# GateLoop and SwiGLU on one core: decays of the first chunks through selection tiles, two units' gates in turns, one weights piece behind the second rows

## The chip, the cores and the metric

One core of a Trainium2 chip runs the whole program. The metric is the device time in microseconds of one execution, as the median of three runs. TensorE is PE in the profile, VectorE DVE, ScalarE ACT, GpSimd POOL, and SyncE (which only issues transfers here) SP.

## What is computed

A gated linear recurrence (GateLoop) is followed by a feed-forward layer with a SwiGLU. Four sequences, eight heads, 768 steps, 48 features per head; then 3072 tokens of width 384, with 1536 hidden features.

```
mag = sqrt(a_re**2 + a_im**2)
a = (a_re + i*a_im) * min(mag, 0.999) / (mag + 1e-6)
for t in range(S):
    state = a[t] * state + outer(k[t], v[t])        # per head, complex
    y[t] = q[t] @ real(state)
x = y, heads side by side: (B*S, 384)
xn = x / sqrt(mean(x*x) + 1e-6) * rms_g
out = (silu(xn @ w_gate) * (xn @ w_val)) @ w_out
```

## The kernel before

The 3072 steps are 24 chunks of 128 steps, six to a sequence. Chunks are worked on in units: chunk 0 is unit 0, chunk 1 is unit 1, and from chunk 2 on two chunks make a unit (`UNITS`, L688). Two chunks also make a feed-forward group, of 256 tokens.

`gates(u)` (from L1011) turns the decays of a unit into rotated and scaled q and k. In stages it squares the real and imaginary parts, takes the reciprocal root, multiplies magnitudes up along the chunk by scans (`t4`), takes their reciprocal root (`root`), takes the half angle by Arctan (stage "turn"), sums angles by scans, takes sine and cosine (`turns`), and multiplies k and q by them into `rot`. Six transfers on SP's queue then spread each chunk's `rot` (features of all heads mixed on 128 partitions) to `kq` (96 partitions for a head's real and imaginary part): the chunk's "rows", noted in `moved`. The decay over a whole chunk, one number per feature and head, is `ends`; six more small transfers on SP spread it to `decay`.

ScalarE evaluates by function tables; a change of table is an ACT_TABLE_LOAD in the profile. The functions of the root, the Arctan, and the Sin are in different tables.

`attend(n)` (L1101) is a chunk's attention: scores of `kq` in blocks into two banks of PSUM, masked into `am` by VectorE's COPY_PREDICATED; transposes of k into `kt`; the products of `am` with `ve` (v with padding) and of q with `state`; the new state from `vn` and `kt`, times `decay`. Then the norm: ScalarE squares the output (`sq`), TensorE sums it, VectorE makes `ssv`, GpSimd takes the power (`rs`), TensorE spreads it over the partitions, VectorE multiplies into `xT`. With both chunks' `xT` a group's feed-forward `feed(g, xT)` (L1222) can start: per block, lists of six products with `wg` and with `wv`, Silu into `sg`, a product into `hT`, and last the products with `wo`.

The weights come as 64-bit floats in twelve pieces, through POOL's queue: 0 and 1 are the first of wg and wv, 2 and 3 the second, 4 and 5 the third, 6 to 11 are wo. `fetch` (L905) issues piece i once piece i-2 has landed; a one-element copy into `junk` on POOL marks the landing. `narrow` (L926) makes 32-bit floats of it: one conversion on ScalarE (128 x 1536) and three steps on VectorE, a shift, a masking step, and an addition (the custom operation on 128 x 3072 words). Three places hold raw pieces in turn, so piece 3 takes the place of piece 0, piece 4 that of 1, piece 5 that of 2. `CLEAR = {3: 0}` (L903) also holds piece 3 until the rows of chunk 0 have landed (`cleared`, a small POOL copy into `seen`).

The order of all instructions comes from a planner (`Flow`, `schedule` at L555): each operation has a planned duration, dependencies taken from the memory that it touches, and a due time worked out backwards; on each engine the planner takes the ready operation that is due first. All instructions are emitted at one line (L667), so groups in the profile are told apart by tile names. Where TensorE would be idle in the first 62 us by plan, the planner puts filler products of `rot` into bank 3 (`flow.warm`, L1338).

At the top level (L1298) `gates(0)` and `gates(1)` are recorded one after the other, then the narrowing of all pieces, then the chunks in turn. The functions follow.

Of the kernel before, what the change touches and what calls it, by code (L numbers as in the profile page):

```python
# [18 lines left out]
P = 128  # L19
# [442 lines left out]
class Flow:  # L462
# [9 lines left out]
    turn = 0.0  # L472
    BEGIN = {"SP": 0.8, "ACT": 0.8, "POOL": 0.8}
# [30 lines left out]
    def note(self, op, ap, write):  # L504
        b = self.box(ap)
        if b is None:
            return
        name, p0, p1, lo, hi = b
        if name.startswith("bank"):
            p0, p1, lo, hi = 0, P, 0, 2048  # L510
        kept = []
        for x in self.seen.get(name, ()):
            o, w, q0, q1, l, h = x
            over = q0 < p1 and p0 < q1 and l < hi and lo < h
            if over and (write or w) and o != op["i"]:
                op["deps"].add(o)
            if not (write and p0 <= q0 and q1 <= p1 and lo <= l and h <= hi):
                kept.append(x)
        kept.append((op["i"], write, p0, p1, lo, hi))
        self.seen[name] = kept  # L520

    def add(self, eng, calls, dur, reads=(), writes=(), table=None, land=None, due=None, after=(), behind=(), late=None, mode=None):
        op = dict(i=len(self.ops), eng=eng, calls=calls, dur=dur, deps=set(), table=table, land=land,
                  base=due, late=late, mode=mode, stage=self.stage, behind={o["i"] for o in behind})
# [30 lines left out]
    def schedule(self):  # L555
# [33 lines left out]
        while True:  # L589
# [36 lines left out]
            o = pick[1]  # L626
            waiting[eng].remove(o)
# [8 lines left out]
            if eng == "PE" and self.warm and t < self.warm["until"]:  # L636
# [33 lines left out]
def fast(tc, ctx, qT, kT, v, a_re, a_im, w_gate, w_val, w_out, rms_g, out, H, bad):  # L670
# [209 lines left out]
    for t in banks[4:6]:  # L880
        fill(t, 0.0, eng="DVE")
    dma(gcol, rms_g.rearrange("(c p) -> p c", p=P))
# [20 lines left out]
    CLEAR = {3: 0}  # L903
# [63 lines left out]
    begun = []  # L967
    started = []
# [5 lines left out]
    def way_of(u):  # L974
        return u if u < 2 else 2 + u % 2
# [26 lines left out]
    def load_kq(u, t):  # L1002
        flow.stage = "kq", u
        for name, ap in (("q", qT), ("k", kT)):
            for i, n in enumerate(UNITS[u]):
                dma(t[name][:, :, i * C:(i + 1) * C],
                    ap[n].rearrange("d (h t) -> (d h) t", t=C).rearrange("(j p) t -> p j t", p=P),
                    behind=moved[HOLD] if u > 1 else rows_)
        return t

    def gates(u):  # L1011
# [46 lines left out]

        flow.stage = "turn", u
        act(im, im, AF.Arctan, after=[root])  # L1060
# [28 lines left out]
        for r in range(2 * ND):  # L1089
            dma(decays[way_of(u)][r:D2:2 * ND], ends[:, r % ND, ns[0]:ns[0] + nt], behind=moved[ns[0]])  # L1090
# [10 lines left out]
    def attend(n):  # L1101
# [4 lines left out]
        later = dict(behind=moved[min(n - 1, HOLD)] if n else ())  # L1106
# [191 lines left out]
    gates(0)  # L1298
    gates(1)
# [3 lines left out]
    for n in range(N):  # L1303
        while gated < NU and UNITS[gated][0] <= n:
            gates(gated)
            gated += 1
# [14 lines left out]
    o = 0  # L1321
# [71 lines left out]
```

## Time and profile before

| | |
|---|---|
| runs | 728.84, 729.06, 732.99 us; median 729.06 |
| the profiled execution's own time | 729.62 us |
| its span, first to last instruction | 727.9 us |
| mean granted TensorE clock | 0.99 |
| busy in the span | PE 685.7 us, DVE 471.6, ACT 334.1, POOL 42.0 |

The profile is of one execution. Its page has the busy time of each engine, the span in 40 slices of 18.2 us (a digit is a tenth of the slice), the transfers, and the chain of work that ended last. A timeline line gives start and length in us, engine, operation, the tile written and those read, and in brackets how long the engine stood idle before it and what ended that. "x6" is six instructions run together in a line. A line of a stretch gives its bounds, length, TensorE's busy time, the clock granted to TensorE as a share of full speed, and the transfers' load.

### The profile page before, as it was taken

To read this page: it belongs to the slowest core of one execution; us is meant where nothing else is said; L and a number is where in the kernel's file an instruction comes from. 1 tells how busy PE (TensorE), PEld (TensorE's weight loads), DVE (VectorE), ACT (ScalarE), POOL (GpSimd) and SP (SyncE) were. 2 spreads that over 40 slices of the span, in tenths; PEclk is the share of its full clock that TensorE was granted. 3 is DMA by queue.
4 is the path that set the end of the run, shared out by engine and by line. 5 is a ranking of instruction groups with operands and counts; after the bars stand their busy time and mean duration, and the time that the engine had idled before them with its cause. 6 is when DMAs were issued, how large, how long until landed. Compare 5 with 4: busy or idle time off the path is not lost.

```text
span 727.9 us, 16198 instructions
## 1 busy us (share of the span) xinstructions
PE 685.7 (94%) x6906; PEld 603.7 (83%) x6906; DVE 471.6 (65%) x740; ACT 334.1 (46%) x452; POOL 42.0 (6%) x80
## 2 busy tenths in 40 slices
PE   0579999999999999999999999999999999999996
PEld 0558867877899889889899889889889889889885
DVE  6979988789897887787847737756745234134121
ACT  7649756755656765732923823822821110110010
POOL 6123100001000000000000000000000000000000
PEclk9979999999999999999999999999999999999999
DMA  8797655634545435543722303314303102200000
GB/s 285 226 304 208 193 168 170 184 106 130 170 127 147 153 93 131 171 153 99 189 82 62 97 20 91 97 34 106 81 17 73 55 12 68 65 13 2 23 1 26
DMA packets 104575, 80.64 MB, mean 111 GB/s; under 512 B 42800, under 2 KB 95280, under 8 KB 104496
## 3 DMA queue, kind: packets, MB, share of 16 engines
q1 hardware_dynamic: 100432, 64.99, 32.8%
q0 software_dynamic: 3264, 14.16, 5.5%
q8 instruction: 56, 0.92, 0.5%
q10 hardware_dynamic: 800, 0.39, 0.2%
q14 instruction: 23, 0.19, 0.1%
HBM read 55.84 MB, written 4.72 MB: 83 GB/s over the span
## 4 chain that ended last, share of the span: by engine, by line
PE 87%; DVE 5%; DMA 3%; ACT 2%; SPq 1%; issue 1%; POOL 0%; DVEq 0%; ACTq 0%
PE bank L667 87%; DMA kq<-rot 2%; SPq L667 1%; DVE turns L667 1%; DVE rot L667 1%; DVE wg L667 1%; ACT t L667 1%; DMA in<-in_a_re_dram 1%; ACT turns L667 0%; DVE t L667 0%; DVE wo L667 0%; DVE wv L667 0%; ACT L667 0%; DVE ot L667 0%; DVE in L667 0%
## 5 line engine op out<-in xcount | busy, mean ns | idle before, releaser
L667 PE MATMUL bank<-xT,wg 128*128 128x256 f32 x864 | 199.8, 381 | 1.6 <-DVE xT L667 1.5
L667 PE MATMUL bank<-xT,wv 128*128 128x256 f32 x864 | 199.1, 380 | 0.0
L667 PEld LDWEIGHTS bank<-xT,wg 128*128 128x128 f32 x864 | 163.7, 191 | 24.5 <-DVE xT L667 2.2
L667 PEld LDWEIGHTS bank<-xT,wv 128*128 128x128 f32 x864 | 163.5, 190 | 22.5
L667 PE MATMUL bank<-wo,hT 128*128 128x192 f32 (+1 forms) x576 | 125.8, 362 | 0.4 <-DVE hT L667 0.4
L667 DVE TENSOR_TENSOR hT<-bank,sg 128x512 f32<-128x512 f32 x72 | 49.6, 689 | 114.4 <-PE bank L667 102.0
L667 PEld LDWEIGHTS bank<-wo,hT 128*128 128x128 f32 x576 | 95.6, 191 | 13.7 <-issue 2.5
L667 ACT ACTIVATE sg<-bank 128x512 f32<-128x512 f32 x72 | 42.9, 596 | 132.0 <-PE bank L667 131.4
L667 ACT ACT_TABLE_LOAD x69 | 88.5, 1283 | 11.5 <-DVE rot L667 7.9
L667 ACT ACTIVATE sq<-bank 128x384 f32<-128x384 f32 x24 | 11.8, 490 | 101.2 <-PE bank L667 101.2
L667 DVE TENSOR_TENSOR rot<-kin,turns 128x768 f32<-128x768 f32 x48 | 44.8, 953 | 14.9 <-DMA kq<-rot 14.5
L667 POOL TENSOR_TENSOR rs<-ssv,mhalf 128x1 f32<-128x1 f32 x24 | 17.2, 717 | 575.4 <-DVE ssv L667 575.4
L667 ACT ACTIVATE kt<-bank 128x384 f32<-128x384 f32 x40 | 18.4, 488 | 60.0 <-PE bank L667 59.8
L667 PE MATMUL bank<-sums,hT 128*128 128x192 f32 x240 | 45.0, 329 | 0.0
L667 ACT ACTIVATE turns<-in 128x768 f32<-128x768 f32 (+1 forms) x39 | 29.9, 789 | 21.0 <-DVE rot L667 12.5
L667 PEld LDWEIGHTS bank<-sums,hT 128*128 128x128 f32 x240 | 39.5, 190 | 0.0
L667 PEld LDWEIGHTS bank<-kq 96*32 96x32 f32 x1536 | 30.3, 111 | 10.4 <-issue 7.7
L667 DVE COPY_PREDICATED am<-causal,bank 128x512 f32<-128x512 int32 x48 | 33.3, 722 | 8.4 <-PE bank L667 8.4
L667 DVE TENSOR_TENSOR hT<-hT 128x768 f32<-128x768 f32 x40 | 38.2, 954 | 0.9
L667 PE MATMUL bank<-am,ve 128*32 128x128 f32 x768 | 38.1, 281 | 0.0
L667 PE MATMUL bank<-kq 96*32 96x96 f32 (+3 forms) x1536 | 34.7, 238 | 3.6 <-DMA kq<-rot 3.6
L667 PE MATMUL bank<-rot 128*128 128x128 f32 x64 | 11.7, 342 | 24.8 <-DVE rot L667 24.8
(112 smaller groups left out, 750.5 us busy)
## 6 DMA issues: line engine op xcount, KB each, us to landing
kq<-rot SPq DMA_DIRECT2D x144, 128.0 KB, 2.4
kin<-in_q_dram SPq DMA_DIRECT2D x24, 192.0 KB, 2.8
kin<-in_k_dram SPq DMA_DIRECT2D x24, 192.0 KB, 3.6
wo<-in_w_gate_dram SPq DMA_DIRECT2D x6, 768.0 KB, 4.6
out_dram<-ot SPq DMA_DIRECT2D x24, 192.0 KB, 2.3
wo<-in_w_val_dram SPq DMA_DIRECT2D x6, 768.0 KB, 5.7
wo<-in_w_out_dram SPq DMA_DIRECT2D x6, 768.0 KB, 5.4
in<-in_a_re_dram SPq DMA_DIRECT2D x11, 384.0 KB, 4.6
```

The costliest lines, as they stand in the source:

```text
L667: fn(*args, **kw)
```

## The change

- The decays of chunks 0 and 1 no longer go by transfers. `ends` of the chunk is multiplied by a small 0/1 tile (`head`) into `own`, three products with the selection tile `pick` spread it to 96 partitions in bank 0 or 1, and VectorE copies it to `decay`. The tiles lie in `ot0` and `ot1`, which are written first by the feed-forward; they are made at the start, by a fill and three copies on POOL and two reductions on VectorE. Other units keep the six transfers.
- `gates` becomes a generator that stops once, ahead of the Arctan; for units 0 and 1 both first parts are recorded, then both second parts, and the Arctan waits for both roots (`roots[-2:]`).
- `CLEAR` is `{3: 1}`: piece 3 waits for the rows of chunk 1.
- The planner: loads of q and k of a unit, and of v of a chunk, form groups whose members don't depend on each other; ScalarE and VectorE may wait a little for an operation that is due over 50 us earlier (`patient`); fillers are planned only once the operations that they wait for are placed.

```diff
+    patient = ("ACT", "DVE")
...
-            if over and (write or w) and o != op["i"]:
+            if over and (write or w) and o != op["i"] and (not op["group"] or self.ops[o]["group"] != op["group"]):
                 op["deps"].add(o)
...
+            if eng in self.patient:
+                for x in waiting[eng]:
+                    if t < ready[x["i"]] < t + o["dur"] - 0.2 and x["due"] < o["due"] - 50.0 and ready[x["i"]] < t + 1.5:
+                        pick = None
+                        free[eng] = max(free[eng], min(ready[y["i"]] for y in waiting[eng] if t < ready[y["i"]]))
+                        break
+                if pick is None:
+                    continue
...
-            if eng == "PE" and self.warm and t < self.warm["until"]:
+            if eng == "PE" and self.warm and t < self.warm["until"] and all("end" in x for x in self.warm["after"]):
...
+    pick = ots[0][:, 0:ND * D2].rearrange("p (r x) -> p r x", r=ND)
+    band, head = (ots[1][:, o:o + n] for o, n in ((0, P // H), (16, H)))
+    own = [ots[1][:, o:o + ND * H].rearrange("p (r h) -> p r h", r=ND) for o in (32, 64)]
+    fill(pick, 0.0, late=LATE)
+    for o, order in ((band, "p (x h) -> p x h"), (head, "p (x h) -> p h x")):
+        add("DVE", [(nc.vector.tensor_reduce, (), dict(out=o, in_=ident.rearrange(order, h=H), axis=mybir.AxisListType.X,
+                                                       op=ALU.add))], 0.3, [ident], [o], late=LATE)
+    for r in range(ND):
+        o = pick[:, r].rearrange("p (x j) -> p x j", j=2 * ND)[:, :, r::ND]
+        copy(o, band.unsqueeze(2).to_broadcast([P, P // H, 2]), eng="POOL", late=LATE)
...
-    CLEAR = {3: 0}
+    CLEAR = {3: 1}
...
+    def send_decays(u):
+        ns = UNITS[u]
+        if u < 2:
+            tt(own[u], ends[:, :, u:u + 1].to_broadcast([P, ND, H]), head.unsqueeze(1).to_broadcast([P, ND, H]))
+            ps = banks[u][0:D2, 0:H]
+            mms([(ps, pick[:, r], own[u][:, r], r == 0, r == ND - 1) for r in range(ND)], 0.5)
+            copy(decays[u][:, :, 0], ps)
+            return
+        for r in range(2 * ND):
+            dma(decays[way_of(u)][r:D2:2 * ND], ends[:, r % ND, ns[0]:ns[0] + len(ns)], behind=moved[max(ns[0], 1)])
...
+        roots.append(root)
+        yield
         flow.stage = "turn", u
-        act(im, im, AF.Arctan, after=[root])
+        act(im, im, AF.Arctan, after=roots[-2:])
...
-        for r in range(2 * ND):
-            dma(decays[way_of(u)][r:D2:2 * ND], ends[:, r % ND, ns[0]:ns[0] + nt], behind=moved[ns[0]])
+        send_decays(u)
...
-    gates(0)
-    gates(1)
+    firsts = [gates(0), gates(1)]
+    for x in firsts * 2:
+        next(x, None)
```

The remaining lines pass the groups on (`group=("kq", u)`, `group=("v", n)`) and run the later units' generators to their end.

More of the change, by code (lines that the diff above doesn't have):

```diff
@@ L514, in note @@
             over = q0 < p1 and p0 < q1 and l < hi and lo < h
-            if over and (write or w) and o != op["i"]:
+            if over and (write or w) and o != op["i"] and (not op["group"] or self.ops[o]["group"] != op["group"]):
                 op["deps"].add(o)
-            if not (write and p0 <= q0 and q1 <= p1 and lo <= l and h <= hi):
+            if op["group"] or not (write and p0 <= q0 and q1 <= p1 and lo <= l and h <= hi):
                 kept.append(x)
@@ L520, in note, with add @@
         self.seen[name] = kept
-    def add(self, eng, calls, dur, reads=(), writes=(), table=None, land=None, due=None, after=(), behind=(), late=None, mode=None):
+    def add(self, eng, calls, dur, reads=(), writes=(), table=None, land=None, due=None, after=(), behind=(), late=None, mode=None, group=None):
         op = dict(i=len(self.ops), eng=eng, calls=calls, dur=dur, deps=set(), table=table, land=land,
-                  base=due, late=late, mode=mode, stage=self.stage, behind={o["i"] for o in behind})
+                  base=due, late=late, mode=mode, group=group, stage=self.stage, behind={o["i"] for o in behind})
         self.ops.append(op)
@@ L967, in fast @@
     begun = []
+    roots = []
     started = []
@@ L1007, in load_kq @@
                     ap[n].rearrange("d (h t) -> (d h) t", t=C).rearrange("(j p) t -> p j t", p=P),
-                    behind=moved[HOLD] if u > 1 else rows_)
+                    behind=moved[HOLD] if u > 1 else rows_, group=("kq", u))
         return t
+    def send_decays(u):
[8 more added lines that the diff above has]
+            dma(decays[way_of(u)][r:D2:2 * ND], ends[:, r % ND, ns[0]:ns[0] + len(ns)], behind=moved[max(ns[0], 1)])
     def gates(u):
@@ L1105, in attend @@
         vv = vns[0]
-        later = dict(behind=moved[min(n - 1, HOLD)] if n else ())
+        later = dict(behind=moved[min(n - 1, HOLD)] if n else (), group=("v", n))
         rows = v[n * C:(n + 1) * C, :].rearrange("t (m e d) -> t m e d", e=2, d=D)
@@ L1304, in fast @@
         while gated < NU and UNITS[gated][0] <= n:
-            gates(gated)
+            list(gates(gated))
             gated += 1
```

## The prediction

> **What bounds the kernel now.** I read the page's slices first, then the chain that ended last.
>
> ```profile
> PE   0579999999999999999999999999999999999996
> DVE  6979988789897887787847737756745234134121
> ...
> PE 87%; DVE 5%; DMA 3%; ACT 2%; SPq 1%; issue 1%; POOL 0%; DVEq 0%; ACTq 0%
> ```
>
> TensorE is full from the fourth slice on, and 87% of the chain is TensorE. So the end is "when the first feed-forward group starts" plus TensorE's remaining work, and a change of the opening counts only by the moment at which that group starts and by gaps after it. By stretches TensorE idles 1.3 us between 80 and 120 us and about 2 us between 120 and 700. The timeline gives the start and what leads to it:
>
> ```profile
> 26.64 3.82 SPq L667 DMA_DIRECT2D decay<-ends  x6
> ...
> 34.40 0.71 DVE L667 COPY_PREDICATED am<-causal,bank 128x512 f32<-128x512 int32 x1
> 35.01 1.77 DVE L667 CUSTOM_DVE_ANT_0 wv<-wo,wv 128x3072 uint16<-128x3072 uint16 x1
> ...
> 38.69 0.55 DVE L667 TENSOR_TENSOR state<-bank,decay 96x384 f32<-96x384 f32 x1 [1.91 <-DMA kq<-rot]
> ...
> 44.56 1.32 DVE L667 COPY_PREDICATED am<-causal,bank 128x512 f32<-128x512 int32 x2
> ...
> 50.40 0.49 ACT L667 ACTIVATE sq<-bank 128x384 f32<-128x384 f32 x1 [3.65 <-PE bank L667]
> ...
> 52.47 0.16 DVE L667 TENSOR_SCALAR ssv<-bank 128x1 f32<-128x1 f32 x1 [2.74 <-PE bank L667]
> ...
> 52.71 1.20 POOL L667 TENSOR_TENSOR rs<-ssv,mhalf 128x1 f32<-128x1 f32 x1 [6.83 <-DVE ssv L667]
> ...
> 55.97 3.21 PEld L667 LDWEIGHTS bank<-xT,wg 128*128 128x128 f32 x12
> ```
>
> The group starts at 55.97, when chunk 1 is normalised. Before that VectorE masks chunk 1's scores (44.56), and VectorE sat nearly full: from 22.3 to 44.56 it idled 0.71 us (30.35 to 31.06) and 1.91 us ahead of `state`, some 2.6 us. That second gap is named kq, but kq of chunk 0 had landed by 28.6; `state` also needs decay0, six small transfers behind each other on SP. Chunk 1's kq landed at 42.62 (chain: "37.42 5.20 DMA kq<-rot"), two us before its mask could run. Hence VectorE, not the rows, sets the opening.
>
> **The change, part by part.** I set the changed program's order, with what each instruction waits for, against these durations.
>
> *Decays by products.* Off SP go twelve transfers: 3.82 us (x6) and later 6.46 us (5.27 + 1.19). On come, per chunk, one small VectorE multiply (0.2, nearest row `ends` 0.15 to 0.17), three TensorE passes (0.3) and one copy (0.15). VectorE pays 0.35 each, and the 1.91 wait goes.
>
> *Two units in turns.* Both arctans now follow both roots, so the table load between them (1.28) goes, but unit 0 waits for unit 1. Walking ScalarE and VectorE: ScalarE takes both units' real parts before unit 0's imaginary square, so unit 0's sum starts at 8.12 instead of 7.47; its scans end at 12.1 (before 10.5). `in,mid` is ahead of the root and needs POOL's `mid`, at 11.17 before; a fill (0.33) and three copies (0.2 to 0.3) ahead make it 12.2. Root u0 12.75, square, root u1 14.3, load, arctan u0 15.6 (before 13.0). Then Copy, first weights piece (1.59), Abs, load (1.28), two sines: the cosine is ready at 22.2 (before 20.42). From there VectorE has no gap, in the order built: turns 0.95, rot 1.85, `in` 0.5, copy 0.1, piece 0's first two steps 2.65, turns 0.95, rot 1.85, piece 0's last 1.75, two masks 1.4, piece 1 2.65, state 0.5, its last 1.7, piece 2 4.45, ssv 0.1: 21.4. Chunk 1's mask starts at 43.6, before 44.56: **1.0 us earlier**. Without the shared turns unit 1 would be late again, as the 42.62 shows.
>
> *Rows and fillers.* kq0 goes out from 24.15 and lands at 30.2 (28.55 before); kq1 is issued from 30.7, behind four ve transfers, and lands at 36.6. Neither is waited for by VectorE (masks at 32.8 and 43.6). Fillers rise from 32 to 43: the 19 ahead of kq0 are 38 passes, 13 at 0.27 (4.21 us for the first 18) and 25 at 0.129 (1.53 for 12): 24.1 to 30.8, 0.6 past the rows, still under VectorE's 32.8. If that cover were gone they would cost the 0.6.
>
> *Piece 3 behind the second rows.* Its transfer starts at 37.0 instead of 29.33. Flights of these 1536 KB were 8.2 (37.34 to 45.5), 9.0, 11.6 (44.26 to 55.9) and 13.2 us; nearest are the two of this stretch, so it lands at 45.2 to 46. ScalarE converts it until 47.7, ahead of chunk 1's square. On VectorE its first two steps (0.95 + 1.76) now stand **before** chunk 1's ssv, where before ssv came first; ssv, then POOL's power, then xT wait behind them.
>
> *From the mask to the start.* The products begin 2.07 after the mask as before (44.56 to 46.63), at 45.7. They took 3.64 at half clock here, and the same list took 2.0 at 96.4 to 98.4. The rows that decide:
>
> ```profile
> 42.60:43.70 1.10, 0.99 (x58) 1.00 1.04 394
> 43.70:46.00 2.30, 1.11 (x24) 0.53 1.12 269
> 46.00:50.00 4.00, 4.00 (x68) 0.50 1.11 299
> ```
>
> (us, length, TensorE busy, granted clock.) Idle began at 40.2 and the clock fell at 43.7, 3.5 later. Now 14 fillers keep TensorE busy to 42.3, so by the row the clock falls at 45.8 and the products end at 49.35. The Trainium skill (TensorE: Matmul & The Clock Gate, "Part 1: The HAM clock gate") says the window of about 3.4 us runs free, so the fall may come up to a window later: by that rule the end lies between 47.7 and 49.35. From the end come transposes (0.55 warm, 0.75 half), decay products and copy (0.45), two steps of piece 3 (2.7): ssv at 51.4 full, 53.3 half. From ssv to the start was 55.97 - 52.47 = 3.5. So the start is 54.9 at full clock and 56.8 at half; without piece 3 ahead the half case would give ssv at 50.6 and a start at 54.1. I take 55.6, a little on the full side of the middle because of the denser fillers: **0.4 us gained**.
>
> *A rule against the change.* The skill (SBUF — State Buffer, "SBUF: two separate sides" and "Who interferes with whom") says VectorE operations with a doubled port, or two SBUF inputs, lock POOL out, and descriptors of POOL's transfers then wait. The row: four selects took 1.29 us at 3.08 and 2.59 at 6.25, when VectorE ran. Four selects, a fill and a copy now precede the first weights' transfer: 1.8 later by the first row, 3.1 by the rule's. Piece 0 then lands at 15.8 or 17.2, and ScalarE takes it at 17.8: nothing either way. For piece 3, under VectorE's steps, the rule's side is a flight of 11.6 or 13.2; that is the rival below.
>
> *Moved with them, at no cost:* grouped kq and v loads no longer wait for each other; kin and ve of units ahead are not waited for in the trace. The planner's new patience (ScalarE and VectorE held for a more urgent operation) adds no instruction; it is in the order that I walked, as the two units' steps ahead of piece 0. Later orders differ in few places: two table loads less, four wo products moved before the last wv list (their piece was ready at 77.1, they run at 84). From the start to unit 2's rows VectorE has the same list both times: piece 4's two steps (2.71) come after instead of before, unit 2's first two (2.71) before instead of after; so the gain passes on.
>
> Sum on the profiled run: 729.62 - 0.4 = 729.2; the median of the runs lies 0.56 lower, so **728.7 us**.
>
> **Rivals.**
> - *More is gained* (0.2): the clock holds (54.9), `mid` doesn't delay (0.6), and the 1.3 us of TensorE gaps between 80 and 120 close with the wo products as cushion: 1.1 + 0.6 + 1.3 = 3.0, 726.1. For it: rows come six us earlier. Against: VectorE's list is no shorter.
> - *Slower, piece 3 late* (0.2): in flight 13.2 from 37.0, seen at 50.4; converted by 52.0; the square behind it 52.5, transposed copy 53, sum and ssv 53.7, start 57.2: 1.2 lost, 730.3. It decides from a conversion end of 55.97 - 5.2 = 50.8, a flight over 12.0. For it: the 11.6 of piece 5. Against: 8.2 and 9.0 in the like stretch.
> - *Nothing moves* (0.1): the decay wait was hidden by the rows anyway; 729.1.
> - *A later stage stalls* (0.05): the new order sends one unit's rows late by several us in a full TensorE: 737 or more. For it: order changes reach the end. Against: TensorE's list is nearly the same.
>
> **How the numbers follow.** The first case has 0.45, its own range 727.7 to 730.1 (starts of 54.9 and 56.8, -1.1 and +0.8 against 55.97, with 0.2 of spread). Rivals one to three all lie within 726 to 731; 725.5 to 732 leaves out the stall and some of the best. About 1%, 7.3 us, is what can be told from no change; only the stall reaches it, and a gain of that size would need a start at 48.7, before the mask has been multiplied: faster 0.02, same 0.93, slower 0.05.
>
> **What would show it.** Right: no idle ahead of `state`; mask of chunk 1 near 43.6; ssv of chunk 1 behind two steps of piece 3; start at 55 to 56; granted clock 0.5 for part of 46 to 50. Wrong: an idle VectorE between 22 and 43 (then rows, table or weights bind), piece 3 seen after 49, or TensorE gaps after 60 that differ by more than 1 us.

## The result, and the profile after

The changed kernel takes 734.32 us (median of 20 runs, 730.09 to 736.32) against 728.95 for the kernel before (20 runs, 727.02 to 735.09): ratio 1.0062, interval 1.0043 to 1.008. It is slower, by less than 1%, and 2.3 us above the top of the predicted range. The profiled execution took 735.89, its span is 734.1.

The page after, in the same order as before:

```profile
PE   0669989999999999999999999999999999999996
DVE  7877978777888787875876777655765233234121
...
PE 85%; DVE 7%; DMA 3%; ACT 2%; issue 2%; POOL 1%; SPq 0%; DVEq 0%; POOLq 0%
```

TensorE's sixth slice (92 to 110 us) has fallen from 9 to 8, and VectorE's share of the chain has grown from 5 to 7%. The timeline of the changed kernel shows the opening (L676 is the L667 of the kernel before):

```profile
37.13 0.55 DVE L676 TENSOR_TENSOR state<-bank,decay 96x384 f32<-96x384 f32 x1
...
38.20 2.07 POOL L676 COPY seen<-kq 96x1 f32<-96x1 f32 x1 [6.50 <-DMA kq<-rot]
40.20 0.78 POOL L676 DMA_DIRECT2D wo<-in_w_val_dram  x1
...
44.32 1.34 DVE L676 COPY_PREDICATED am<-causal,bank 128x512 f32<-128x512 int32 x2
...
50.47 0.96 DVE L676 TENSOR_SCALAR wv<-wo 128x1536 int32<-128x1536 int32 x1 [1.25 <-DMA wo<-in_w_val_dram]
51.50 1.77 ACT L676 ACTIVATE wo<-wo 128x1536 int32<-128x1536 uint32 x1 [4.54 <-POOL junk L676]
...
53.02 0.63 ACT L676 ACTIVATE sq<-bank 128x384 f32<-128x384 f32 x1
...
55.63 0.16 DVE L676 TENSOR_SCALAR ssv<-bank 128x1 f32<-128x1 f32 x1 [2.40 <-PE bank L676]
55.70 1.75 DVE L676 CUSTOM_DVE_ANT_0 wv<-wo,wv 128x3072 uint16<-128x3072 uint16 x1
55.88 2.00 POOL L676 TENSOR_TENSOR rs<-ssv,mhalf 128x1 f32<-128x1 f32 x1 [3.66 <-DVE ssv L676]
...
59.45 5.43 PE L676 MATMUL bank<-xT,wg 128*128 128x256 f32 x12 [0.29 <-DVE xT L676]
```

`state` no longer waits (1.91 us before), and the mask of chunk 1 runs at 44.32 instead of 44.56. But piece 3 is issued at 40.20, behind the small `seen` copy (96 x 1), which takes 2.07 us here. It lands at 50.45; on ScalarE its conversion (51.50 to 53.27) stands ahead of chunk 1's square, on VectorE its steps stand ahead of `ssv`. The square comes 2.6 us later than before, `ssv` 3.2 later, and TensorE's first feed-forward list starts at 59.45, against 56.18 before: 3.3 late. That list takes 5.43 us for 3.40 before: the granted clock from 49 to 60 us is 0.59 here, against 0.77.

That is half of what the end shows: the span grew by 6.2. The rest appears at the second feed-forward group. It needs chunks 2 and 3; "row 3" is chunk 3, and its rows are the last to land. In the timeline before stand the start of the first group, row 3's rotation on VectorE, the first product of row 3's scores, and the start of the second group:

```profile
56.18 3.40 PE L667 MATMUL bank<-xT,wg 128*128 128x256 f32 x12
...
92.53 1.82 DVE L667 TENSOR_TENSOR rot<-kin,turns 128x768 f32<-128x768 f32 x2
...
100.13 0.77 PE L667 MATMUL bank<-kq 96*32 96x128 f32 x32 [1.01 <-DMA kq<-rot]
...
118.85 2.86 PE L667 MATMUL bank<-xT,wg 128*128 128x256 f32 x12 [0.32 <-DVE xT L667]
```

The last three after:

```profile
97.81 1.81 DVE L676 TENSOR_TENSOR rot<-kin,turns 128x768 f32<-128x768 f32 x2
...
107.94 0.77 PE L676 MATMUL bank<-kq 96*32 96x128 f32 x32 [3.63 <-DMA kq<-rot]
...
126.65 2.86 PE L676 MATMUL bank<-xT,wg 128*128 128x256 f32 x12 [0.32 <-DVE xT L676]
```

The second group starts 7.8 us late. The chains of waits say when those rows left and how long they flew, before and then after:

```profile
96.05 3.48 DMA kq<-rot
```

```profile
102.00 5.80 DMA kq<-rot
```

They left 5.95 later and flew 2.32 longer, and the product followed the landing by 0.14 instead of 0.60: 7.8. TensorE itself was late there too, but by less: it was ready for this product at 104.31 (3.63 before 107.94) against 99.12, so 5.2 late, 3.3 of it by its start and the rest by the clock, which was low from 51.03 to 64.68 (before, up to 57.48). The later of the two ways, that of the rows, decides. They leave once VectorE has rotated them: the rotation ends 5.3 later (94.35 and 99.62), and the other 0.7 passes between its end and the last sending on SP's queue (1.70 before, 2.38 after). So the stretches of VectorE tell most of the rest. Columns: bounds, length, then the busy time of TensorE, weight loads, VectorE, ScalarE and GpSimd, with instructions in brackets, granted clock, DMA share and GB/s. Before:

```profile
49.00:60.00 11.00, 9.62 (x65) 8.26 (x58) 8.13 (x8) 9.44 (x13) 3.48 (x3) 0.77 0.86 228
60.00:100.00 40.00, 39.12 (x379) 32.57 (x377) 37.95 (x54) 31.41 (x41) 5.94 (x11) 1.00 0.73 222
```

After:

```profile
49.00:60.00 11.00, 6.09 (x26) 5.26 (x26) 5.83 (x9) 8.41 (x13) 3.86 (x4) 0.59 1.07 340
60.00:100.00 40.00, 40.00 (x239) 32.84 (x240) 36.42 (x46) 23.19 (x27) 7.70 (x13) 0.94 0.56 172
```

VectorE's idle time from 49 to 100 us is 8.75 after (5.17 and 3.58) and 4.92 before (2.87 and 2.05). It lost 3.8 us more; the other 1.5 of the rotation's 5.3 are work that the kernel before had behind it by 49 (VectorE is busy for 40.42 us from 49 to the end of the rotation before, 41.87 after). Not all of the 3.8 is lost in the stall itself: 1.70 us of it is a wait at 67.57 for TensorE's first lists, which had started late and at the lower clock; the longest such wait before was 0.98.

### The profile page after: what moved, and what is told of

Read it like the earlier page. It is cut to its first block, busy times and chain, and to the rows that moved or that the text cites. A ratio compares the mean times of both kernels' runs of the same rounds, so it can differ in the third digit from the quotient of the medians.

```text
span 734.1 us, 16261 instructions
## 1 busy us (share of the span) xinstructions
PE 691.7 (94%) x6940; PEld 609.9 (83%) x6940; DVE 474.7 (65%) x746; ACT 332.1 (45%) x450; POOL 48.4 (7%) x84
## 4 chain that ended last, share of the span: by engine, by line
PE 85%; DVE 7%; DMA 3%; ACT 2%; issue 2%; POOL 1%; SPq 0%; DVEq 0%; POOLq 0%
PE bank L676 85%; DMA wo<-in_w_val_dram 1%; DVE wo L676 1%; DVE t L676 1%; DVE rot L676 1%; DVE turns L676 1%; DMA kq<-rot 1%; ACT L676 1%; ACT t L676 1%; DVE wv L676 1%; DMA in<-in_a_re_dram 1%; DVE wg L676 0%; ACT turns L676 0%; ACT in L676 0%; DVE hT L676 0%
## 5 line engine op out<-in xcount | busy, mean ns | idle before, releaser
L676 PE MATMUL bank<-xT,wg 128*128 128x256 f32 x864 | 201.7, 384 | 1.5 <-DVE xT L676 1.5
L676 PE MATMUL bank<-xT,wv 128*128 128x256 f32 x864 | 199.0, 380 | 0.0
L676 PEld LDWEIGHTS bank<-xT,wg 128*128 128x128 f32 x864 | 164.9, 192 | 24.8 <-DVE xT L676 2.2
L676 PEld LDWEIGHTS bank<-xT,wv 128*128 128x128 f32 x864 | 163.7, 190 | 22.9
L676 DVE TENSOR_TENSOR hT<-bank,sg 128x512 f32<-128x512 f32 x72 | 49.7, 690 | 119.5 <-PE bank L676 110.1
L676 PE MATMUL bank<-wo,hT 128*128 128x192 f32 (+1 forms) x576 | 125.8, 362 | 0.4 <-DVE hT L676 0.4
L676 ACT ACTIVATE sg<-bank 128x512 f32<-128x512 f32 x72 | 43.0, 597 | 143.9 <-PE bank L676 143.3
L676 PEld LDWEIGHTS bank<-wo,hT 128*128 128x128 f32 x576 | 95.4, 191 | 13.1 <-issue 1.5
L676 POOL TENSOR_TENSOR rs<-ssv,mhalf 128x1 f32<-128x1 f32 x24 | 21.2, 882 | 571.4 <-DVE ssv L676 571.4
L676 ACT ACTIVATE sq<-bank 128x384 f32<-128x384 f32 x24 | 11.9, 496 | 94.3 <-PE bank L676 92.5
L676 DVE TENSOR_TENSOR rot<-kin,turns 128x768 f32<-128x768 f32 x48 | 44.6, 950 | 11.1 <-DMA kq<-rot 10.6
L676 ACT ACTIVATE kt<-bank 128x384 f32<-128x384 f32 x40 | 18.7, 493 | 58.7 <-PE bank L676 58.4
L676 PE MATMUL bank<-sums,hT 128*128 128x192 f32 x240 | 45.1, 329 | 0.0
L676 PEld LDWEIGHTS bank<-kq 96*32 96x32 f32 x1536 | 29.7, 110 | 12.3 <-issue 10.4
L676 PEld LDWEIGHTS bank<-sums,hT 128*128 128x128 f32 x240 | 39.4, 190 | 0.0
L676 PE MATMUL bank<-kq 96*32 96x96 f32 (+3 forms) x1536 | 34.1, 235 | 5.6 <-DMA kq<-rot 5.6
L676 DVE TENSOR_TENSOR hT<-hT 128x768 f32<-128x768 f32 x40 | 38.1, 954 | 0.8
L676 PE MATMUL bank<-am,ve 128*32 128x128 f32 x768 | 37.1, 275 | 0.0
L676 DVE COPY_PREDICATED am<-causal,bank 128x512 f32<-128x512 int32 x48 | 33.2, 722 | 5.3 <-PE bank L676 5.3
L676 ACT ACTIVATE turns<-in 128x768 f32<-128x768 f32 (+1 forms) x39 | 30.0, 790 | 14.3 <-DVE in L676 10.7
L676 ACT ACTIVATE t<-t 128x768 f32<-128x768 f32 (+1 forms) x39 | 30.9, 794 | 7.8 <-DVE t L676 7.5
```

Source lines behind the costliest of these rows:

```text
L676: fn(*args, **kw)
```

## The experiments

Two theories were put against each other. The first: piece 3 is late, and whoever stands behind it in an in-order queue is late with it; the place of its steps ahead of chunk 1's norm is what costs. The other: some other part of the change (the turns, the decays, the planner's rules, the landing itself) costs by itself; each run's expectation names its rival. Edits to the order are lines put behind `flow.schedule()`, with `of(stage, eng)` the operations of a stage on an engine; nothing else is changed. Each run is set against the kernel before on its own chip, in five rounds.

### Is it the place of piece 3, or its landing?

**Norm first.** The changed kernel with piece 3's conversion, its three steps and its marking copy behind chunk 1's norm, and with them piece 5's issue, which follows that copy; six operations moved, no other.

```diff
+    at = 0.0
+    for eng in ("POOL", "ACT", "DVE"):
+        at = max([at] + [o["order"] for o in of(("norm", 1), eng)])
+        late = [o for o in of(("w", 3), eng) if o["land"] is None]
+        if eng == "POOL":
+            late += [o for o in of(("w", 5), eng) if o["land"] is not None]
+        for o in sorted(late, key=lambda o: o["order"]):
+            if o["order"] < at + 0.5:
+                at += 0.01
+                o["order"] = at
```

> The changed kernel with piece 3 as late as it is, but its GpSimd copy and conversions put behind the norm chain of chunk 1 on GpSimd, ScalarE and VectorE. Theory (it is the place at the head of the queues that costs, not the lateness): piece 3 still lands at 50 us or later, but chunk 1's square comes at 48 in place of 53.0, its sum at 49.5 to 50.5 in place of 55.6, the feed starts at 51.5 to 53.5 us in place of 59.4, and the time falls by what the start falls, to 726 to 729 us. Rival A (turns, planner): 732 or over. Rival C (the weights themselves are too late, the feed starves later): the feed starts early but TensorE then idles in front of piece 3, 4 or 5, and the time stays at 731 or over.

727.01 us, ratio 0.9996 (0.9976 to 1.0016): as expected, the whole loss is gone, and the time is that of the kernel before. Its timeline:

```profile
50.25 0.16 DVE L676 TENSOR_SCALAR ssv<-bank 128x1 f32<-128x1 f32 x1 [0.99 <-PE bank L676]
...
50.49 0.55 POOL L676 TENSOR_TENSOR rs<-ssv,mhalf 128x1 f32<-128x1 f32 x1 [5.32 <-DVE ssv L676]
...
52.31 2.86 PE L676 MATMUL bank<-xT,wg 128*128 128x256 f32 x12 [0.49 <-DVE xT L676]
...
117.72 2.86 PE L676 MATMUL bank<-xT,wg 128*128 128x256 f32 x12 [0.32 <-DVE xT L676]
```

The start is 3.9 us earlier than before, yet the time isn't: TensorE then idles about 5 us in six waits up to the second group, which starts only 1.1 earlier than before. The stretches of this kernel show TensorE's part and VectorE's:

```profile
49.00:60.00 11.00, 10.51 (x62) 9.41 (x61) 8.48 (x14) 8.78 (x12) 3.08 (x4) 1.00 1.06 336
60.00:100.00 40.00, 35.88 (x358) 28.25 (x356) 38.99 (x50) 25.76 (x33) 8.63 (x13) 1.00 0.70 215
```

From 60 to 100 TensorE idles 4.12 us, and yet the second group is no later than before. VectorE idles 3.53 from 49 to 100, 5.2 less than in the changed kernel; row 3's rotation ends at 94.37 instead of 99.62, also 5.2 earlier, and its rows leave at 97.19 instead of 102.00. So the place of the six operations explains the loss, and it reaches the second group as VectorE's time.

**Piece 3 ahead of the second rows**, else as changed.

```diff
+    [piece] = [o for o in of(("w", 3), "POOL") if o["land"] is not None]
+    piece["order"] = cleared[1]["order"] - 0.3
```

> The changed kernel with piece 3's transfer issued ahead of GpSimd's second copy from kq; nothing else moves. Theory (piece 3 lands late and stands at the head of ScalarE's and VectorE's queues, in front of chunk 1's square and sum): the transfer is issued when piece 0's third VectorE step ends, 33.3 us in place of 40.2, and lands near 43, before its readers are free; chunk 1's square no longer waits, group 0's feed starts at 55 to 56.5 us in place of 59.4, and the time is 727 to 730 us. Rival A (the turns of the two units or the planner's order are what costs): the time stays at 732 or over, with the feed's start behind 58. Rival B (the transfer of piece 3 now takes the queues from chunk 1's rows): these rows land at 42 or later in place of 38.1 and chunk 1's mask comes after 45.5 us; 730 to 733.

739.19, 1.0154 (1.0131 to 1.0178): a miss, five more us lost. Its timeline:

```profile
33.74 0.78 POOL L676 DMA_DIRECT2D wo<-in_w_val_dram  x1 [2.19 <-DVE wg L676]
...
43.86 1.30 PE L676 MATMUL bank<-kq 96*32 96x128 f32 x32 [7.76 <-DMA kq<-rot]
```

With the piece in flight from 33.74, chunk 1's scores start at 43.86 instead of 38.19; the mask comes at 46.74 and 47.84, the start at 62.52. So holding piece 3 back does what it says: it clears the way of the rows, by 5.7 us. The late rows aren't the whole price: 30 filler products stand in TensorE's queue ahead of the products with `am` and take from 47.68 to 52.06, so these begin 4.9 us after the second mask, where the changed kernel has 1.6. An earlier landing did not help; that a late one does no harm is shown by the norm-first run, where the piece was issued as late (40.31).

**Both edits together**: the lines of the two diffs, one behind the other; at their end

```diff
+                o["order"] = at
+    [piece] = [o for o in of(("w", 3), "POOL") if o["land"] is not None]
+    piece["order"] = cleared[1]["order"] - 0.3
```

> Both moves on the changed kernel: piece 3's transfer ahead of the second copy from kq, and its conversions behind the norm chain of chunk 1. Theory: the feed starts at 51.5 to 53.5 us as with the second move alone, and the first move adds at most 0.5 us either way, since piece 3 is needed only in the feed's third block, some 13 us after its start; 725.5 to 729 us. Rival C: only this one of the two is fast, since here the weights are early too (726 against 731). Rival B: rows of chunk 1 land at 42 or later and the time is 1 us or more over that of the second move alone.

733.76, 1.008 (1.0051 to 1.0109): a miss again; only the rival "the rows are late" fits. Beside the norm-first run the earlier piece costs 6.7 us (scores at 42.92, fillers from 46.75 to 52.4, start 59.41).

**The kernel before, with piece 3 behind the second rows.**

```diff
+    at = max([o["order"] for o in moved[1]] + [o["order"] for o in of(("w", 3), "POOL") if o["land"] is not None]) + 0.1
+    cleared[1]["order"] = at
+    for i in (3, 4):
+        [o] = [o for o in of(("w", i), "POOL") if o["land"] is not None]
+        o["order"] = max(o["order"], at + 0.1 * i)
```

> The kernel before with one thing of the change: GpSimd's second copy from kq is put ahead of piece 3's transfer, which so starts behind chunk 1's rows; no instruction of another engine moves. Theory: chunk 1's rows land near 38 to 39 in place of 42.7, piece 3 is issued at 39 to 40 in place of 29.3 and lands at 48 to 50; its first VectorE step stands in front of chunk 1's mask there, so the mask comes at 49 to 51 us in place of 44.6, the feed starts at 60 to 62 in place of 56.0, and the time is 733 to 736 us. Rival A (turns, planner's order): this kernel has neither, so it stays at 728.5 to 730.

732.55, 1.0057 (1.0038 to 1.0077): just under the range expected, and the loss of the whole change to within the intervals. Its timeline:

```profile
39.99 0.78 POOL L667 DMA_DIRECT2D wo<-in_w_val_dram  x1
...
48.85 0.96 DVE L667 TENSOR_SCALAR wv<-wo 128x1536 int32<-128x1536 int32 x1 [6.99 <-DMA wo<-in_w_val_dram]
49.73 1.34 DVE L667 COPY_PREDICATED am<-causal,bank 128x512 f32<-128x512 int32 x2
```

Here the late piece stands ahead of the mask itself, and VectorE stands still for 6.99 us. The start is 61.30, 5.1 late; row 3's rows leave at 101.67, 5.6 late. VectorE's busy time up to 100 us is 5.5 us less (80.11 against 85.65): the microseconds lost at 42 to 49 are still missing 50 us later.

**The kernel before, with pieces 3 and 4 behind the norm of chunk 1** (the first edit, for both pieces; against its lines:)

```diff
-        late = [o for o in of(("w", 3), eng) if o["land"] is None]
+        late = [o for i in (3, 4) for o in of(("w", i), eng) if o["land"] is None]
...
-            late += [o for o in of(("w", 5), eng) if o["land"] is not None]
+            late += [o for o in of(("w", 6), eng) if o["land"] is not None]
```

> The kernel before, with the conversions of pieces 3 and 4 and their GpSimd copies put behind chunk 1's norm chain; nothing of the change. Theory: piece 3's first VectorE step (0.95 us) no longer stands in front of chunk 1's mask, and piece 4's in front of xT; chunk 1's mask at 43.6 to 44.0 us in place of 44.56, the feed's start at 53.5 to 55 us in place of 55.97. As the row-3 transfers, and with them what follows 100 us, hang on VectorE's sum of work and not on the start, only a part is kept: 726.5 to 728.5 us. Rival (the start of the first feed fixes the end, as the prediction had it): 725.5 to 726.5.

734.1, 1.0094 (1.0063 to 1.0125): a miss. The start does come earlier, 53.83, but the timeline shows the bill:

```profile
70.66 4.39 PE L667 MATMUL bank<-xT,wv 128*128 128x256 f32 x12 [3.63 <-DVE hT L667]
```

What VectorE puts off is missed later; the second group starts at 121.34, 2.5 late (this was the fastest of its runs, 730.88; what the median lost beyond it isn't in the trace). Putting the norm first is no gain in itself: it saves a wait where the piece is late, and here the pieces weren't.

**The changed kernel with the planner's old rules** (`patient` empty, no groups), in which the norm comes ahead of piece 3 by itself.

```diff
-    patient = ("ACT", "DVE")
+    patient = ()
...
-                    behind=moved[HOLD] if u > 1 else rows_, group=("kq", u))
+                    behind=moved[HOLD] if u > 1 else rows_)
...
-        later = dict(behind=moved[min(n - 1, HOLD)] if n else (), group=("v", n))
+        later = dict(behind=moved[min(n - 1, HOLD)] if n else ())
```

> The changed kernel with the planner's two new rules taken out; decays by products, turns and piece 3's label as changed. Without them the planner puts chunk 1's square, sum and xT in front of piece 3 on all three engines. Theory: no stall in the norm chain, the feed starts at 51.5 to 55 us in place of 59.4, rows of row 3 go out at 95.5 to 99 in place of 102.0, and the time is 726 to 730 us. Rival (decays, turns or the label cost by themselves): 732 or over.

737.31, 1.0125 (1.0106 to 1.0143): a miss by 7 us; of the two expectations only the rival's "732 or over", by which the other parts of the change cost by themselves, fits. The start is 53.24, as the theory says, so an order with the norm ahead isn't enough. The second group starts at 122.18 in the profiled execution, but that was the fastest of its runs (733.22), and the rest of the median's loss isn't in it. This stays open.

### Which start does the end follow?

Over all profiled kernels, the span minus the start of the second group is 606.8 to 609.2 us; minus the start of the first it is 669 to 679. Four runs tested this by adding work whose results nobody uses, so the output isn't touched.

**A late start without VectorE lost**: the norm-first kernel with 28 more filler products on TensorE ahead of the first group.

```diff
+    row = min(of(("feed", 0), "PE"), key=lambda o: o["order"])
+    row["calls"] = flow.warm["call"] * 28 + row["calls"]
```

> The second experiment's kernel with 28 more passes on TensorE (128x128, results not used) put in front of feed 0's first list: at some 0.137 us each 3.8 us, of which 0.5 us fill a wait, so that the feed starts at 55 to 56 us in place of 52.3; VectorE's work is the same. Theory (VectorE's path comes last here): TensorE's idle of 5 us between the two feeds' starts takes up most of it, feed 1 moves by 0 to 1.2 us, and the time is 727 to 728.2 us. Rival (the start fixes the end): feed 1 at 120.5 to 121.5, 729.5 to 730.5 us.

728.72, 0.9992 (0.9973 to 1.001). The start is 57.31, 5.0 us later than in the norm-first kernel; the time is the same. The chain of waits and the timeline:

```profile
97.18 3.28 DMA kq<-rot
```

```profile
119.51 2.86 PE L676 MATMUL bank<-xT,wg 128*128 128x256 f32 x12 [0.32 <-DVE xT L676]
```

Row 3's rows leave at the same moment (97.19 without the edit), and the first product of its scores comes at 100.60 instead of 100.69. That the second group still starts 1.8 later is the clock, which fell in this execution and not in the other (last section).

**VectorE lost without a late start**: the norm-first kernel with a fill and three products of 128 x 768 on VectorE behind chunk 1's `xT` (measured 0.70 + 2.94 us).

```diff
+    [row] = [o for o in of(("norm", 1), "DVE") if o["order"] == max(x["order"] for x in of(("norm", 1), "DVE"))]
+    idle = sums.rearrange("p a b -> p (a b)")[:, 0:768]
+    row["calls"] = row["calls"] + [(nc.vector.memset, (idle, 0.0), {})] + [
+        (nc.vector.tensor_tensor, (), dict(out=idle, in0=idle, in1=idle, op=ALU.mult))] * 3
```

> The second experiment's kernel (piece 3 behind the norm chain, 727.0 us) with extra work of no use on VectorE right behind chunk 1's xT: one fill and three products of 128x768, some 3.3 us (a product of this size took 0.95 us). The feed's start is not touched (52.3 us). Theory (two paths lead to feed 1, and with an early start it is VectorE's sum of work up to the rotation of row 3 that comes last): the rows of row 3 go out 2.5 to 3.5 us later than 97.2 us, feed 1 starts at 120 to 121.5 in place of 117.7, and the time is 729 to 730.5 us. Rival (the start of feed 0 fixes the end, as the prediction had it): 726.5 to 727.5.

731.43, 1.004 (1.0012 to 1.0069). The start is 52.37, unmoved; the chain and the timeline:

```profile
100.31 3.98 DMA kq<-rot
```

```profile
123.14 2.86 PE L676 MATMUL bank<-xT,wg 128*128 128x256 f32 x12 [0.32 <-DVE xT L676]
```

3.64 us held at 54 become 3.1 at the sending of the rows and 5.4 at the second group (3.1, plus 0.6 of flight, plus 1.7 by the clock, below). This pair tells the two apart in this order: 5.0 us at the start of the first group change the time by nothing that can be measured, 3.6 us of VectorE by 2.7 us (731.43 against 728.72, both on one chip), most of what they last.

**The same two on the kernel before.** VectorE held, by the lines just shown:

```diff
+    row["calls"] = row["calls"] + [(nc.vector.memset, (idle, 0.0), {})] + [
+        (nc.vector.tensor_tensor, (), dict(out=idle, in0=idle, in1=idle, op=ALU.mult))] * 3
```

> The kernel before with the same 3.3 us of extra VectorE work right behind chunk 1's xT; feed 0's start stays at 56.0 us. TensorE waited 1.0 us for row 3's rows already. Theory: both paths are nearly level in this kernel, so VectorE's delay is passed on too: row 3's rows go out at 98.5 to 99.5 in place of 96.05, feed 1 starts at 121 to 122.5, and the time is 730 to 731.5 us. Rival (only the start counts): 727.5 to 728.5.

730.38, 1.0023 (1.0002 to 1.0044); start 56.35, rows out at 100.18 (4.1 late), second group 121.29 (2.4 late, since the clock, which fell before, held here). A late start, by 16 products:

```diff
+    row["calls"] = flow.warm["call"] * 16 + row["calls"]
```

> The kernel before with 16 more passes on TensorE (results not used) in front of feed 0's first list, 2.2 us at full clock and up to 4.3 at the half clock that stands there, so that the feed starts at 57.5 to 60 us in place of 56.0. In the kernel before TensorE idles only 1.3 us between the two feeds' starts. Theory: here the start counts nearly in full; feed 1 moves by the start's delay less at most 1.3 us, to 119.5 to 121.5 in place of 118.85, and the time rises by as much, to 728.5 to 730.5 us. If VectorE's path alone counted here too: 727.5 to 728.2.

735.93, 1.007 (1.0035 to 1.0105): a miss in size, and no clean test. The fillers in front, these and those planned before, took 5.83 us at a granted clock of 0.78, chunk 1's v was late as well (TensorE waited 1.88 for it), and VectorE, which in this order waits for TensorE's lists, was only 34.74 us busy from 60 to 100 (37.95 before). The start is 61.93, 5.75 late, and row 3's rows leave at 101.79, 5.74 late: here the late start passed on in full, with the second group at 126.42. So whether a late start costs depends on the order: it was free in the norm-first order, where VectorE's list doesn't stand still for it, and not in this one. Which of the two the changed kernel's own order resembles was not tried.

**Row 3's rotation earlier**: the norm-first kernel with that chunk's two rotation steps right behind those of the chunk ahead of it.

```diff
+    rows3 = sorted(of(("rot", 2), "DVE"), key=lambda o: o["order"])[-2:]
+    rows2 = sorted(of(("rot", 2), "DVE"), key=lambda o: o["order"])[-3]
+    for k, o in enumerate(rows3):
+        o["order"] = rows2["order"] + 0.01 * (k + 1)
```

> The second experiment's kernel (727.0 us) with the two VectorE steps of row 3's rotation (1.81 us) put right behind those of row 2, in front of four weight steps and two of the state. Theory: row 3's rows go out and land 2 to 4 us earlier (100.6 in place of 100.6 less that much only if SP is free), while the weights of the last products come 1.8 us later, for which TensorE waited 0.85 us already; the gain is what remains, feed 1 at 115.5 to 118 in place of 117.7 and 725 to 727.5 us. Rival (VectorE's whole sum up to feed 1's xT counts, not the place of the rotation): 726.5 to 728.5.

731.89, 1.0042 (1.0028 to 1.0057): a miss for both sides. In the timeline the wait has only moved:

```profile
93.20 2.92 PE L676 MATMUL bank<-wo,hT 128*128 128x384 f32 x4 [2.59 <-DVE wo L676]
...
103.62 1.30 PE L676 MATMUL bank<-kq 96*32 96x128 f32 x32 [2.70 <-DMA decay<-ends]
```

The rows no longer decide; the weights of wo and this unit's decays, which VectorE makes after them, do. The second group starts at 123.67, 6.0 later than with the norm first: 2.9 by these waits, 3.0 by the clock (20.1 us from row 3's scores for 17.0).

### What the other parts are worth

Each of these lets the planner make a new order, so they aren't clean single parts.

**No turns**: each unit's gates recorded whole, Arctan behind its own root.

```diff
-        act(im, im, AF.Arctan, after=roots[-2:])
+        act(im, im, AF.Arctan, after=roots[-1:])
...
-    for x in firsts * 2:
-        next(x, None)
+    for x in firsts:
+        list(x)
```

> The changed kernel with the gates of units 0 and 1 recorded one after the other, as before; decays and piece 3 as changed, so the planner again puts piece 3's conversion in front of chunk 1's square on ScalarE and two of its VectorE steps in front of chunk 1's sum. Theory (place of the late piece at the head of the queues): the stall stays, piece 3 lands at 47 to 51 us, the feed starts at 57 or later, and the time is 731 to 736 us. Rival A (the turns are what costs): the stall is gone or harmless without them, the start is 54 to 56.5 and the time 727 to 729.5 us.

730.21, 1.0036 (1.0016 to 1.0055), between the two expectations. The stall is still there (piece 3 seen at 48.96, `ssv` 54.17, power 2.00, start 57.68), yet the second group starts at 119.20, 0.4 later than before. With the norm put first as well (the lines of the first edit, and these):

```diff
-    for x in firsts * 2:
-        next(x, None)
+    for x in firsts:
+        list(x)
```

> The changed kernel without the turns, and with piece 3's conversions and GpSimd copy behind chunk 1's norm chain. It stands to e3 as the second experiment stands to the changed kernel, and to the second experiment as one part, the turns, alone. Theory: the start returns to 51.5 to 54.5 us and the time to 726 to 729 us; the turns alone are worth at most 1 us either way. Rival A (the turns cost): 1.5 us or more below the second experiment's 727.0. Rival D (the turns gain what VectorE waited): 729 us or over.

731.06, 1.0039 (1.0016 to 1.0061): a miss; the rival by which the turns gain fits. Each run stands against the kernel before on its own chip, so the ratios compare: taking the turns out gains some 1.9 us in the order with the stall (1.0062 to 1.0036) and loses some 3.1 in the order without it (0.9996 to 1.0039), and in both cases the intervals touch. What the turns are worth by themselves isn't settled.

**Decays by transfers again**, else as changed.

```diff
-        if u < 2:
+        if u < 0:
...
-            dma(decays[way_of(u)][r:D2:2 * ND], ends[:, r % ND, ns[0]:ns[0] + len(ns)], behind=moved[max(ns[0], 1)])
+            dma(decays[way_of(u)][r:D2:2 * ND], ends[:, r % ND, ns[0]:ns[0] + len(ns)], behind=moved[ns[0]])
```

> The changed kernel with the decays of the first two chunks spread by transfers as before; turns and piece 3 as changed. In this order the planner happens to put chunk 1's square, sum and xT in front of piece 3's conversion on ScalarE; on VectorE only piece 3's first step stands ahead of xT. Theory: the six transfers put between the two chunks' rows on SP cost these rows 3 to 4 us (six issues of some 0.6 us), so chunk 1's mask comes at 45 to 48 us; but chunk 1's square does not wait for piece 3 and the feed starts at 53 to 57 us; 727 to 731 us, faster than the changed kernel. Rival (the products themselves, or rather their set-up on GpSimd, delay the opening): at or below 727 us with chunk 0's mask at least 1 us earlier than 33.2 us. If the place at the head of the queues were not the cause: 733 or over.

730.02, 1.0028 (1.0006 to 1.0049). The planner's order then has `ssv` of chunk 1 at 48.14, ahead of piece 3, and the earliest start of all kernels; its timeline:

```profile
50.85 2.86 PE L676 MATMUL bank<-xT,wg 128*128 128x256 f32 x12 [0.27 <-DVE xT L676]
...
87.70 1.56 PE L676 MATMUL bank<-wo,hT 128*128 128x384 f32 x4 [2.02 <-DVE wo L676]
```

A start 5.3 us earlier than before, and no time gained: TensorE waits for VectorE instead, and the second group starts at 121.32.

**The planner's new rules alone, on the kernel before** (`patient` and the groups, as in the diff of the change; its heads:)

```diff
+    patient = ("ACT", "DVE")
...
-            if over and (write or w) and o != op["i"]:
+            if over and (write or w) and o != op["i"] and (not op["group"] or self.ops[o]["group"] != op["group"]):
...
+            if eng in self.patient:
```

> The kernel before with the planner's two new rules only (ScalarE and VectorE may wait for a far more urgent step; transfers of a group are not ordered among themselves); decays, turns and piece 3's label as before. The rules put piece 0's third VectorE step behind chunk 0's mask, where it reads the room that piece 3 is loaded to. Theory: piece 3's transfer is so issued at 33 us or later in place of 29.3 and travels beside chunk 1's rows, as in the first experiment; these rows land at 42 or later, its conversion stands in front of chunk 1's square, and the time is 730 to 736 us. Rival (the rules by themselves cost nothing): 727 to 729.5 us.

734.38, 1.0073 (1.005 to 1.0096): as expected, the new rules alone cost as much as the whole change. The timeline:

```profile
33.27 1.74 DVE L676 CUSTOM_DVE_ANT_0 wg<-wo,wg 128x3072 uint16<-128x3072 uint16 x1
...
35.57 1.21 POOL L676 DMA_DIRECT2D wo<-in_w_val_dram  x1 [5.27 <-DMA kq<-rot]
...
43.37 1.77 POOL L676 COPY seen<-kq 96x1 f32<-96x1 f32 x1 [6.60 <-DVE wg L676]
```

VectorE is held for chunk 0's mask, so piece 0's last step runs at 33.27, the place of piece 0 comes free late, and piece 3 leaves at 35.57 instead of 29.33. The start is 58.22, the second group 127.63.

No version beat both kernels: norm first equals the kernel before.

## Why the prediction was wrong

*The decay wait* (1.91 us goes, `state` unhindered): right. *The mask of chunk 1 one us earlier, at 43.6*: it came at 44.32, 0.24 gained. The cosine was ready at 22.87 for the predicted 22.2; the walk of 21.4 us from there was right, for it took from 22.91 to 44.32. (The 0.71 us that VectorE is said to have idled at 30.35 before weren't idle: its step from 29.38 lasted to 31.14.) *Rows of chunk 0 and 1 not waited for by VectorE*: right; chunk 1's landed at 38.1 for 36.6.

*Piece 3* was the first step that failed: "it lands at 45.2 to 46". It landed at 50.45. Of the 4.5 to 5.3 us, 1.5 are the rows' later landing, and 1.3 to 2.1 are the flight of 10.25. The other 1.7 are the `seen` copy: the prediction left 0.4 from the rows' landing to the issue, and the copy alone took 2.07 beside VectorE's steps. The place of its steps was read rightly, "before chunk 1's ssv", and that made every microsecond of lateness count.

*Products at 45.7, done at 47.7 by the rule's side or 49.35 by the row's*: they ran 45.88 to 47.85 at full clock, the rule's side. But the clock fell at 51.03, while TensorE waited behind piece 3, and stayed low under the first lists; the sum has no term for that. *ssv to the start, 3.5*: 3.8, the power having grown from 1.20 to 2.00 beside VectorE's custom operation. *The start, 55.6*: 59.45. The rival "piece 3 late" saw the piece "at 50.4" (it was 50.47), but by luck: it had a flight of 13.2 from 37.0, and the trace has 10.25 from 40.20. It gave 57.2; the conversion ended at 53.27 instead of 52.0 and it took 6.2 from there, not 5.2. Its mechanism was right; a chance of 0.2 and 730.3 us weren't.

*The rule against the change* (SBUF — State Buffer): it was looked for at the descriptors of the flight, where the prediction gave it as a flight of 11.6 or 13.2 (measured 10.25); it bit at the copy ahead of the flight and at the power. The prediction also read the page too widely: for two SBUF inputs the page names only GpSimd's reads, and the wait of descriptors only for the doubled port.

The second step that failed is the sum itself: "So the end is 'when the first feed-forward group starts' plus TensorE's remaining work". The end follows the start of the second group, with 606.8 to 609.2 us behind it in all kernels. The late-start run moved the first by 5.0 us at an unchanged time, the held VectorE lengthened the time with an unmoved first, and the earliest start of all (50.85) gave a slower kernel. The first start is still one of the ways to the second: in the order of the kernel before, 5.75 us of it passed on in full, and in the changed kernel TensorE's own way was 5.2 us late at row 3's scores, the rows' way 7.8. What the sum left out is VectorE's way to row 3's rows, on which it had little room, about 3.5 to 5 us idle in 51. With it fails "so the gain passes on": there was a loss, 3.8 us of VectorE's time and 1.5 of work left over, and it passed on to row 3's rows. The rival "a later stage stalls" names that mechanism ("sends one unit's rows late by several us in a full TensorE"); it was set aside because "TensorE's list is nearly the same". VectorE's list was compared too, and called the same; how long VectorE would stand still in it was not. That the norm-first edit alone, six operations moved, takes the loss away is shown, and with it that a piece as late as this does no harm by its landing as such.

Open: the worth of the turns, which has either sign by the order around them; the loss with the old rules, about half of which the profiled execution doesn't show; and why row 3's rows flew 5.80 us after where the kernel before and the norm-first, held-VectorE, late-start and piece-behind runs have 3.07 to 3.98. The transfers' load during the flight was 0.95 after and 0.64 to 0.84 in those; what filled it was not tried.

## What to carry to other kernels

When a transfer is put later, list every engine's instructions that wait for it and what stands behind them in the queue: put ahead of them what doesn't need the data and is due sooner, and count what that puts off (on the kernel before it cost 0.9%). A bound on TensorE late in the kernel doesn't make its first start the clock: look for the last point at which the full engine waits for another, and count backwards along that other engine, whose lost time may surface 50 us later. Compare not only its list of work but where it will stand still. And a fetch that is moved forward again may cost more, where small urgent transfers share its time.

## What the runs showed of the hardware

*Tiny operations on GpSimd.* The `seen` copy (96 x 1) took 0.19 us at 45.59 before, and 2.07, 2.39 and 2.48 in the changed, norm-first and held-VectorE kernels, where VectorE's wide steps ran beside it. Of the 34 such copies in the 17 profiles 28 took 0.30 us or more, and each of these ends 0.04 or 0.05 us behind the end of a VectorE instruction; the other six took 0.18 to 0.20. The power took 0.55 to 0.57 alone and 2.00 beside the custom operation, ending 0.43 behind it. So the small operation waits VectorE's instruction out. That agrees with the Trainium skill (SBUF — State Buffer, "Who interferes with whom"), by which a VectorE instruction in a doubled-port mode, or one with two SBUF inputs against a GpSimd instruction that reads SBUF, shares its ports with GpSimd, and one blocks for the whole of the other; the runs add that a transfer issued behind the copy waits with it.

*The clock behind short gaps.* From the first product of row 3's scores to the second group took 17.0 us where the clock stayed at 1.00, 18.7 to 18.9 where it fell for 3.4 us, and 20.1 and 20.3 (row 3's rotation earlier, and the kernel before with a late start) where it stayed down for 6.8. Before, a gap of 1.01 us was followed by a fall; the stretch:

```profile
100.00:104.00 4.00, 3.87 (x43) 2.70 (x44) 3.11 (x6) 0.68 (x2) 0.56 (x1) 0.73 0.19 22
```

Without the turns a gap of 2.28 us was not, in these two stretches:

```profile
100.00:104.00 4.00, 1.83 (x40) 1.63 (x41) 1.90 (x5) 0.94 (x4) 0.00 (x0) 1.00 0.57 133
104.00:108.00 4.00, 4.00 (x45) 2.46 (x44) 4.00 (x5) 2.41 (x4) 0.56 (x1) 1.00 0.38 104
```

The length of the gap alone doesn't decide. Half-microsecond stretches give the moments at which the clock changes, worked out with 0.50 as the low clock. Before, it falls at 43.82, rises at 50.65, falls at 54.06, rises at 57.48, falls at 101.85 and rises at 105.26: the distances are 6.83, 3.41, 3.42, 44.37 and 3.41 us, within 0.01 all multiples of 3.413. In seven other profiles (those of the changed kernel, piece 3 ahead, VectorE held, both late starts, row 3's rotation earlier and the old rules) the changes keep the same step. So in these runs the clock changes only at ticks 3.41 us apart, whatever the program does in between, and one such stretch at half clock costs a full TensorE half of it, the 1.7 us above. The Trainium skill (TensorE: Matmul & The Clock Gate, "Part 1: The HAM clock gate") states this window, free-running and 3413 ns long, and the traces agree. Where the ticks fall may be why the norm-first kernel's runs lie in two clumps, 725.7 to 727.7 at a mean granted clock of 0.995 to 0.999 and 729.4 to 732.2 at 0.991 to 0.995; this was not tested.
